# The mean of V from fp32 sums on GpSimd and one fp32 product, in a clustered-attention and MoE kernel

## The chip, the core and the metric

The kernel runs on one core of a Trainium2 chip. The metric is the device time of one execution in microseconds (us), the median of several runs. Engines are called as in the profile: PE is TensorE's matmul, PEld its weight load, DVE VectorE, ACT ScalarE, POOL GpSimd, SP SyncE, whose queue issues nearly all DMAs.

## The reference

Two batches of eight heads, 768 positions, head size 64. Queries and keys are each put into one of 16 clusters, and a query only sees keys of its own cluster. Where a query's cluster holds no key, every score is the same large negative number, and the softmax becomes the plain mean of V over all 768 positions. That is the mean in question.

```python
mask = q_assign[:, :, :, None] == k_assign[:, :, None, :]
scores = np.where(mask, scale * np.matmul(q, k.transpose(0, 1, 3, 2)), -1e9)
scores = scores - np.max(scores, axis=-1, keepdims=True)
attn = np.exp(scores)
attn = attn / (np.sum(attn, axis=-1, keepdims=True) + 1e-09)
x = np.matmul(attn, v)                 # then heads side by side: 1536 x 512
h = x @ w_in;   x = act1(h) @ w_out    # two feed-forward layers, 512 -> 2048 -> 512
h = x @ w2_in;  out = (s * relu(h) ** 2 + b) @ w2_out
```

## The kernel before

Heads go in eight pairs p (numbers 0 to 7), two heads of 64 columns side by side. The attention is a list of 96 slots t, six for each head, twelve for each pair; each slot handles 128 keys of a head. All engines run their instructions in the order in which the program issues them, and the order of a slot is written by hand in `slot(t)`: one half of the row maxima (`max_mm`, PE, L747), the DMAs of the slot (SP), the scores (`scores`, PE, L812 and L813), the other half of the maxima, the exponentials (`probs`: ACT makes `ph` in fp16 and `pf` in fp32 at L823 and L824, and POOL the rest `pl = pf - ph` at L826), the products with V of the slot before the last (`values(t - 2)`, PE, L842, which read `ph`, `pl` and V), then what the tables `steps` and `extra` hold for this slot. So `pl(t)` is wanted by PE two slots after its own.

V of a pair comes as `rv`, one buffer for all pairs (`load_v`, L475, in pool `rvp` with one buffer), 128 partitions of 2 heads x 6 pieces j x 64 columns. `scale_v` (L618) takes the largest magnitude, `peak_row` and `peak_all` (L630 to L651) carry it across partitions with a small fp32 product against the table `eye`, `scale_v2` makes the power of two `sc` and, with `iv` (L665), its inverse divided by 768. `split_v` (ACT, L673) and `split_v2` (DVE, L677) write V times `sc` as an fp16 pair `vh`, `vl`. When these are done, the one buffer `rv` is free, and the load of the next pair may go.

`mean(p)` stands in slot 12p + 7 (`PX`), behind that slot's `values`: twelve fp16 products of a 128x128 block of ones with `vh` and `vl` of the six pieces, summed in PSUM (L689, L690), and in the next slot two scaled copies by ACT, one for each head (L695). `no_match(p)` puts the mean where a query has no key, much later. `peak_all` of an odd pair stands in the same slot as the mean of the pair before, right behind it on PE. After slot 95 come the two feed-forward layers, products of 512 columns on PE to the end.

Of the kernel before, what the change touches and what calls it, by code (L numbers as in the profile page):

```python
# [8 lines left out]
F32 = mybir.dt.float32  # L9
# [4 lines left out]
ACTF = mybir.ActivationFunctionType  # L14
ALU = mybir.AluOpType
# [10 lines left out]
def clustered_attention_moe_kernel(  # L26
# [24 lines left out]
    nc = tc.nc  # L51
    B, H, S, D = q.shape
# [3 lines left out]
    J = S // 128  # L56
# [44 lines left out]
    def bank(kind, name):  # L101
        return banks[kind].tile([128, TB], F32, tag=kind, name=name)
# [3 lines left out]
    half, one, s_col, b_col, low = (cols[:, i:i + 1] for i in range(5))  # L106
# [251 lines left out]
    for n, w in enumerate(loadq[len(early):]):  # L358
        start, pace = PACES[w[0]]
# [47 lines left out]
    def attention(es, prep):  # L407
        def pool(name, bufs, stack=es):
            side = "left" if stack is prep else "right"
            return stack.enter_context(tc.tile_pool(name=name, bufs=bufs, side=side))  # L410
# [8 lines left out]
        acon = pool("acon", 1)  # L419
        ccon = pool("ccon", 1, prep)  # L420
        smp = pool("smp", 4)
        vp = pool("vp", 2)
# [3 lines left out]
        ident = acon.tile([128, 128], F32, name="ident")  # L426
        ones16 = acon.tile([128, 128], F16, name="ones16")
# [1 line left out]
        firsts = acon.tile([128, 128], F16, name="firsts")  # L429
        level = acon.tile([128, 2], F32, name="level")  # L430

        eye = acon.tile([2, 4], F32, name="eye")


        CW = 96 + 128 * HP
# [5 lines left out]
        raw, halves, sims, ohts, vt, heads, pr = {}, {}, {}, {}, {}, {}, {}  # L441
# [3 lines left out]
        def spare():  # L445

            if spares:
                spares.append(spares.pop(0))
                return bank(spares[-1], spares[-1] + "b")
            return bank("x", "xb")  # L450
# [174 lines left out]
        def peak_row(p):  # L625
            st = {}

            def pe():
                st["ps"] = spare()[0:2, 0:128]
                nc.tensor.transpose(st["ps"], vt[p][0], ident)  # L630

            def dve():
                mx = smp.tile([2, 1], F32, tag="pk", name="pk")
                nc.vector.tensor_reduce(out=mx, in_=st["ps"], axis=AX.X, op=ALU.max)
                ex = smp.tile([2, 1], I32, tag="ex", name="ex")

                nc.vector.tensor_scalar(
                    out=ex, in0=mx.bitcast(I32), scalar1=0x7F800000, scalar2=None, op0=ALU.bitwise_and
                )
                nc.vector.tensor_scalar(out=ex, in0=ex, scalar1=float(27 << 23), scalar2=None, op0=ALU.max)  # L640
                vt[p] = [ex.bitcast(F32)]

            return pe, None, dve

        def peak_all(p):
            st = {}

            def pe():
                st["ps"] = spare()[:, 0:4]
                ex = vt[p][0]  # L650
                nc.tensor.matmul(st["ps"], lhsT=ex.to_broadcast([2, 128]), rhs=eye, start=True, stop=True)  # L651

            def dve():
                scale_v2(p, st["ps"])

            return pe, None, dve

        def scale_v2(p, ex):

            sc = vp.tile([128, 2], I32, tag="sc", name="sc")  # L660
            nc.vector.tensor_scalar(
                out=sc, in0=ex[:, 0:2].bitcast(I32), scalar1=-1.0, scalar2=float(268 << 23), op0=ALU.mult, op1=ALU.add
            )
            iv = vp.tile([128, 2], F32, tag="iv", name="iv")
            nc.vector.tensor_copy(iv, ex[:, 2:4])  # L665
            vh = vp.tile([128, 2, J, D + 1], F16, tag="vh", name="vh")
            vl = vp.tile([128, 2, J, D], F16, tag="vl", name="vl")
            nc.gpsimd.memset(vh[:, :, :, D:D + 1], 1.0)
            vt[p] = [vh, vl, sc.bitcast(F32), iv, None]

        def split_v(p, e):
            vh, vl, scf, ivf, _ = vt[p]
            nc.scalar.activation(out=vh[:, e, :, 0:D], in_=raw[p, "v"][:, e], func=ACTF.Copy, scale=scf[:, e:e + 1])  # L673

        def split_v2(p, e):
            vh, vl, scf, ivf, _ = vt[p]
            nc.vector.scalar_tensor_tensor(  # L677
                out=vl[:, e], in0=raw[p, "v"][:, e], scalar=scf[:, e:e + 1], in1=vh[:, e, :, 0:D],
                op0=ALU.mult, op1=ALU.subtract,
            )  # L680

        def mean(p):
            st = {}

            def pe():
                vh, vl = vt[p][0:2]
                ps = st["ps"] = spare()[:, 0:2 * D].rearrange("p (h d) -> p h d", h=2)
                for j in range(J):
                    nc.tensor.matmul(ps, lhsT=ones16, rhs=vh[:, :, j, 0:D], start=(j == 0), stop=False)  # L689
                    nc.tensor.matmul(ps, lhsT=ones16, rhs=vl[:, :, j, :], start=False, stop=(j == J - 1))  # L690

            def act():
                mv = vp.tile([128, 2, D], F32, tag="mv", name="mv")
                for e in range(2):
                    nc.scalar.activation(  # L695
                        out=mv[:, e], in_=st["ps"][:, e], func=ACTF.Copy, scale=vt[p][3][:, e:e + 1]
                    )
                vt[p][4] = mv

            return pe, act  # L700

# [162 lines left out]
        def no_match(p):  # L864

            nm = spare()[:, 0:2 * J].rearrange("p (h j) -> p h j", h=2)
            nc.scalar.activation(out=nm, in_=heads.pop((p, "mx")), func=ACTF.Relu, scale=-1.0, bias=low)
            nc.vector.copy_predicated(
                out=heads[p, "x"],
                mask=nm.bitcast(I32).rearrange("p h j -> p j h")[:, :, :, None].to_broadcast([128, J, 2, D]),  # L870
                data=vt[p][4][:, None].to_broadcast([128, J, 2, D]),
            )

        def x_out(p, n):
            b, hp = divmod(p, HP)
            j0, j1 = PIECE[n]
            xs = slice(b * S + j0 * 128, b * S + j1 * 128)
            st = {}

            def pe():  # L880
                x = heads[p, "x"]
                ps = st["ps"] = spare()[:, 0:(j1 - j0) * 128]
                for j in range(j0, j1):
                    nc.tensor.transpose(
                        ps[:, (j - j0) * 128:(j - j0 + 1) * 128], x[:, j, :, :].rearrange("p h d -> p (h d)"), ident
                    )

            def act():
                nc.scalar.activation(out=xt_h[:, hp, xs], in_=st["ps"], func=ACTF.Copy)

            def dve():
                nc.vector.tensor_tensor(  # L892
                    out=xt_l[:, hp, xs], in0=st["ps"], in1=xt_h[:, hp, xs].bitcast(F32), op=ALU.subtract
                )

            return pe, act, dve
# [32 lines left out]
        steps, extra, mid, dmas = {}, {}, {}, {}  # L929

        def at(d, t, f, *a):
            d.setdefault(t, []).append((f, a))

        def step(t, x):
            steps.setdefault(t, []).append(x)

        for g in range(1, NH // 4):
            z = 24 * g
            for a, at_load, places in ((0, 46, PT[0:4]), (1, 34, PT[4:8])):
                p = 2 * g + a  # L940
# [10 lines left out]
        for p in range(NP):  # L951
            z = 12 * p
            zl, za, zs, zh, zg = PV[p % 2][0:3] + (PV[p % 2][3:5], PV[p % 2][5:7])
            if p != 1:
                at(dmas, z + zl + int(p == NP - 1), load_v, p)
            at(*((extra, z - 8) if p in (1, NP - 1) else (mid if p % 2 else extra, z + za)), scale_v, p)
            step(z + zs[0], peak_row(p))
            step(z + zs[1], peak_all(p))
            for e in range(2):
                at(extra, z + zh[e], split_v, p, e)  # L960
                at(extra, z + zg[e], split_v2, p, e)
            zx = PX[p % 2]
            step(z + zx[0], mean(p))
            if p < NP - 1:
                step(z + zx[1], x_out(p, 0))
                step(z + zx[2], x_out(p, 1))
# [91 lines left out]
        def turn2(p, nm, aside, *kinds):  # L1058
            spares[:] = kinds
            whole(turn(p, nm, 0, aside), turn(p, nm, 1, aside))  # L1060
# [58 lines left out]
        for x in (s0, s1):  # L1119
            x[0](((1, 1),))  # L1120
        s0[2]()
        s1[2]()
        nc.vector.tensor_copy(eye[:, 0:2], ident[0:2, 0:2])
        nc.vector.tensor_scalar(
            out=eye[:, 2:4], in0=ident[0:2, 0:2], scalar1=2.0 ** -14 / S, scalar2=None, op0=ALU.mult
        )
        turn2(2, "q", True, "s")
        turn2(2, "k", True, "m")
        warm(9)
# [41 lines left out]
        for e in range(2):  # L1171
            lead(J + e, ("ms", "sm")[e])
            split_v2(0, e)
# [9 lines left out]
    with tc.manual_schedule():  # L1183
        with ExitStack() as es, ExitStack() as prep:
            attention(es, prep)
        ff_pools(("wc", NWC))
        for n in range(TAIL, len(units) + 2):
            ff_step(n)
# [33 lines left out]
```

## Time and profile before

| | |
|---|---|
| median of 3 runs | 768.39 us (767.7 to 769.45) |
| profiled execution, span from first to last instruction | 766.2 us |
| mean granted TensorE clock | 0.997 of 2.4 GHz |
| PE busy | 747.7 us (98%), 5019 products |
| DVE busy | 483.3 us (63%) |
| ACT busy | 472.9 us (62%) |
| POOL busy | 318.3 us (42%) |

The page gives the profiled execution's span alone; the timed runs are about 2 us longer, which is what lies around the span. Shares of busy time are means over the attention (to about 240 us) and the feed-forward layers, which have different limits.

### The profile page before, as it was taken

Reading aid. Unit: us, or ns where it says so; the run is one execution under the profiler, and the core shown is the slowest. Engines: PE = TensorE matmul, PEld = TensorE weight load, DVE = VectorE, ACT = ScalarE, POOL = GpSimd, SP = SyncE. Lnnn points to the kernel's source line nnn. Section 1 sums busy time; section 2 is a strip of 40 time slices with the busy share of each in tenths; the row PEclk is TensorE's granted clock in tenths of the full one; section 3 lists DMA queues with packets and bytes.
Section 4 is the critical chain, followed back from the end, with each engine's and each line's share of the span. In section 5 each row is a group of like instructions: output and inputs, shape, how many; then the busy total and the mean of one; then the engine's idle time right before and its main releaser. Section 6 shows DMA issues by size and latency. Waiting matters only on the chain.

```text
span 766.2 us, 13218 instructions
## 1 busy us (share of the span) xinstructions
PE 747.7 (98%) x5019; PEld 622.5 (81%) x5019; DVE 483.3 (63%) x871; ACT 472.9 (62%) x949; POOL 318.3 (42%) x242
## 2 busy tenths in 40 slices
PE   8899999999999999999999999999999999999998
PEld 5678888988877787888888888888888888888886
DVE  6889898898887968885464349889932222222222
ACT  5389799898997777777466247866643333333332
POOL 4388688687885463555043004655630000000000
PEclk9999999999999999999999999999999999999999
DMA  9777657376511443443022003434400100010001
GB/s 199 166 154 167 142 111 174 93 162 165 134 55 58 137 138 111 137 138 111 0 84 83 0 1 119 136 103 142 133 1 1 55 1 1 0 56 1 0 1 55
DMA packets 59887, 67.52 MB, mean 88 GB/s; under 512 B 29008, under 2 KB 47536, under 8 KB 59824
## 3 DMA queue, kind: packets, MB, share of 16 engines
q1 hardware_dynamic: 59792, 66.63, 33.3%
q8 instruction: 39, 0.64, 0.4%
q14 instruction: 24, 0.20, 0.1%
q10 hardware_dynamic: 32, 0.05, 0.0%
HBM read 43.03 MB, written 3.15 MB: 60 GB/s over the span
## 4 chain that ended last, share of the span: by engine, by line
PE 83%; DVE 9%; DMA 3%; ACT 3%; issue 1%; SPq 0%; DVEq 0%; ACTq 0%
PE y L302 33%; PE h L241 32%; PE o L842 4%; PE m L747 3%; PE s L812 3%; PE s L813 3%; DVE rowmax L758 3%; PE xb L544 1%; DVE vl L677 1%; DMA rv<-in_v_dram 1%; DMA kb<-oht 1%; ACT ph L823 1%; DMA rk<-in_k_dram 1%; ACT pf L824 1%; PE xb L491 1%
## 5 line engine op out<-in xcount | busy, mean ns | idle before, releaser
L241 PE MATMUL h<-xt_h,w 128*128 128x512 f32 x768 | 252.9, 390 | 0.5 <-ACT w L179 0.4
L826 POOL TENSOR_TENSOR pl<-pf,ph 128x768 f16<-128x768 f32 x94 | 156.8, 1674 | 50.8 <-ACT pf L824 22.6
L241 PEld LDWEIGHTS h<-xt_h,w 128*128 128x128 f32 x768 | 144.1, 188 | 30.8 <-ACT w L179 0.8
L241 PE MATMUL h<-xt_l,w 128*128 128x512 f32 x384 | 149.6, 390 | 0.0
L277 POOL TENSOR_TENSOR gl<-g,gh 128x512 fp32r<-128x512 f32 x51 | 66.8, 1309 | 182.2 <-ACT gh L275 177.5
L275 ACT ACTIVATE gh<-g 128x512 fp32r<-128x512 f32 x96 | 60.4, 630 | 106.5 <-PE y L302 66.7
L823 ACT ACTIVATE ph<-s 128x384 f16<-128x384 f32 x192 | 102.1, 532 | 29.9 <-PE s L813 28.6
L302 PE MATMUL y<-gh,w 128*128 128x512 f32 x384 | 108.5, 390 | 1.2 <-DVE t L163 1.0
L758 DVE TENSOR_REDUCE rowmax<-m 128x1 f32<-128x384 f32 x180 | 95.4, 549 | 15.8 <-PE m L747 14.7
L302 PE MATMUL y<-w,gh 128*128 128x512 f32 x384 | 105.2, 389 | 0.0
L824 ACT ACTIVATE pf<-s 128x384 f32<-128x384 f32 x192 | 103.5, 539 | 0.0
L270 DVE TENSOR_SCALAR g<-g,cols 128x512 f32<-128x512 f32 x48 | 27.5, 573 | 100.8 <-ACT g L261 100.6
L302 PEld LDWEIGHTS y<-gh,w 128*128 128x128 f32 x384 | 72.0, 188 | 17.8 <-DVE t L163 1.4
L241 PEld LDWEIGHTS h<-xt_l,w 128*128 128x128 f32 x384 | 72.1, 188 | 14.9 <-DVE xt_l L892 0.2
L302 PEld LDWEIGHTS y<-w,gh 128*128 128x128 f32 x384 | 72.0, 188 | 15.0
L180 POOL TENSOR_TENSOR w<-t,w 128x512 fp32r<-128x512 f32 x64 | 83.1, 1309 | 0.0
L260 ACT ACTIVATE g<-h 128x512 f32<-128x512 f32 x48 | 28.6, 596 | 78.2 <-PE h L241 76.3
L747 PE MATMUL m<-kb,qb 80*128 80x384 f32 x180 | 68.4, 381 | 2.6 <-DVE rowmax L758 2.1
L277 DVE TENSOR_TENSOR gl<-g,gh 128x512 fp32r<-128x512 f32 x45 | 31.2, 693 | 62.5 <-ACT gh L275 62.5
L842 PEld LDWEIGHTS <-ph 128*128 128x128 f16 x1152 | 54.8, 98 | 19.0 <-issue 13.5
L812 PE MATMUL s<-qa,ka 128*128 128x384 f32 x192 | 66.7, 347 | 0.2 <-ACT pf L824 0.2
L813 PE MATMUL s<-qb,kb 128*128 128x384 f32 x192 | 65.0, 338 | 1.9 <-DMA qb<-mr 1.9
(195 smaller groups left out, 1304.4 us busy)
## 6 DMA issues: line engine op xcount, KB each, us to landing
raw<-in_moe_w_in_dram SPq DMA_DIRECT2D x32, 512.0 KB, 3.7
raw<-in_moe_w_out_dram SPq DMA_DIRECT2D x32, 512.0 KB, 3.3
rq<-in_q_dram SPq DMA_DIRECT2D x16, 192.0 KB, 4.4
rk<-in_k_dram SPq DMA_DIRECT2D x16, 192.0 KB, 4.9
rv<-in_v_dram SPq DMA_DIRECT2D x8, 384.0 KB, 5.3
out_dram<-o SPq DMA_DIRECT2D x12, 256.0 KB, 2.3
qb<-qh SPq DMA_DIRECT2D x14, 192.0 KB, 3.2
kb<-kh SPq DMA_DIRECT2D x14, 192.0 KB, 3.8
```

Of the source, the lines that this page charges most:

```text
L180: nc.gpsimd.tensor_tensor(out=l, in0=f, in1=h.bitcast(F32), op=ALU.subtract)
L241: nc.tensor.matmul(h_t[m, t, c], lhsT=w[:, kk * 128:(kk + 1) * 128], rhs=x[:, kk, tokens(t)], start=((n, kk) == H_PARTS[0]), stop=((n, kk) ...
L277: eng.tensor_tensor(out=gl, in0=g, in1=gh.bitcast(F32), op=ALU.subtract)
L302: nc.tensor.matmul(y[i], lhsT=ops[n][0], rhs=ops[n][1], start=(begin and n == 0), stop=(end and n == 2))
L747: nc.tensor.matmul(ps, lhsT=hd["qb"][0:NQ, j * 128:(j + 1) * 128], rhs=hd["kb"][0:NQ, n * S // 2:(n + 1) * S // 2], start=True, stop=True,)
L758: nc.vector.tensor_reduce(out=hd["m2"][:, j, n:n + 1], in_=mst.pop((u, n)), axis=AX.X, op=ALU.max)
L812: nc.tensor.matmul(ps, lhsT=hd["ka"][:, cs], rhs=hd["qa"][:, qs], start=True, stop=False)
L813: nc.tensor.matmul(ps, lhsT=hd["kb"][:, cs], rhs=hd["qb"][:, qs], start=False, stop=True)
L823: nc.scalar.activation(out=ph[:, qs], in_=ps, func=ACTF.Exp, scale=qk_scale)
L824: nc.scalar.activation(out=pf[:, qs], in_=ps, func=ACTF.Exp, scale=qk_scale)
L826: eng.tensor_tensor(out=pl, in0=pf, in1=ph, op=ALU.subtract)
L842: nc.tensor.matmul(o[:, j, 0:w], lhsT=lhsT[:, js], rhs=rhs[:, e, c, :], start=(c == 0 and j == 0 and x == 0), stop=(c == J - 1 and j == J ...
```

## The change

The mean no longer comes from the fp16 pair. `sum_v(p)` adds the six raw fp32 pieces of `rv` on POOL: five additions of 128 x 128 elements, the sum `vs` kept in place, in one buffer for all pairs. It stands in `extra` of slot 12p - 5, for pair 0 in slot 0, so behind that slot's `pl` in POOL's order. `mean(p)` stays in its slot, as a single fp32 product of a column of ones, broadcast to 128x128, with `vs`; ACT then makes one copy of 128x128 with the constant scale 1/768 in place of two. `iv` and its DVE copy go, and with them two of the four columns of `eye` and of `peak_all`'s product, and one small DVE instruction in the set-up.

```diff
-        eye = acon.tile([2, 4], F32, name="eye")
+        eye = acon.tile([2, 2], F32, name="eye")
...
-                st["ps"] = spare()[:, 0:4]
+                st["ps"] = spare()[:, 0:2]
...
-            iv = vp.tile([128, 2], F32, tag="iv", name="iv")
-            nc.vector.tensor_copy(iv, ex[:, 2:4])
...
+        def sum_v(p):
+            r = raw[p, "v"]
+            vs = raw[p, "vs"] = smp.tile([128, 2, D], F32, tag="vs", name="vs", bufs=1)
+            for j in range(1, J):
+                nc.gpsimd.tensor_tensor(out=vs, in0=vs if j > 1 else r[:, :, 0], in1=r[:, :, j], op=ALU.add)
+
         def mean(p):
...
-                for j in range(J):
-                    nc.tensor.matmul(ps, lhsT=ones16, rhs=vh[:, :, j, 0:D], start=(j == 0), stop=False)
-                    nc.tensor.matmul(ps, lhsT=ones16, rhs=vl[:, :, j, :], start=False, stop=(j == J - 1))
+                nc.tensor.matmul(
+                    ps, lhsT=one.to_broadcast([128, 128]), rhs=raw.pop((p, "vs")), start=True, stop=True
+                )
...
-                for e in range(2):
-                    nc.scalar.activation(
-                        out=mv[:, e], in_=st["ps"][:, e], func=ACTF.Copy, scale=vt[p][3][:, e:e + 1]
-                    )
+                nc.scalar.activation(out=mv, in_=st["ps"], func=ACTF.Copy, scale=1.0 / S)
...
+            at(extra, max(0, z - 5), sum_v, p)
...
-        nc.vector.tensor_copy(eye[:, 0:2], ident[0:2, 0:2])
-        nc.vector.tensor_scalar(
-            out=eye[:, 2:4], in0=ident[0:2, 0:2], scalar1=2.0 ** -14 / S, scalar2=None, op0=ALU.mult
-        )
+        nc.vector.tensor_copy(eye, ident[0:2, 0:2])
```

## Rows read from the trace of the kernel before

**Rows 1.** The page: busy time, share of the span and instructions of each engine.

```profile
PE 747.7 (98%) x5019; PEld 622.5 (81%) x5019; DVE 483.3 (63%) x871; ACT 472.9 (62%) x949; POOL 318.3 (42%) x242
```

**Rows 2.** Busy time by stretch: the attention's slots; us, busy (instructions), clock, DMA share, GB/s.

```profile
32.00:240.00 208.00, 200.38 (x2595) 174.77 (x2594) 178.76 (x388) 181.66 (x461) 160.86 (x104) 1.00 0.58 132
```

**Rows 3.** Groups by line and form: count | busy us, mean ns | idle before them.

```profile
L826 POOL TENSOR_TENSOR pl<-pf,ph 128x768 f16<-128x768 f32 x94 | 156.8, 1674 | 50.8 <-ACT pf L824 22.6 <-PE s L813 10.7 <-PE m L747 7.8
...
L689 PE MATMUL xb<-vh,ones 128*128 128x128 f16 x48 | 6.3, 220 | 0.0
...
L512 POOL TENSOR_TENSOR w<-rq,w 128x768 fp32r<-128x768 f32 x1 | 1.8, 1835 | 2.4 <-ACT rq L506 2.4
...
L665 DVE COPY iv<-xb 128x2 f32<-128x2 f32 x7 | 1.1, 150 | 0.0
```

**Rows 4.** The chain of waits around slots 19 to 21: start us, us, what.

```profile
75.33 0.06 PE xb L689
...
76.00 0.23 PE m L747
...
77.69 0.31 PE xb L651 x2
78.00 0.38 PE m L747
...
79.81 0.47 PE xb L491 x4
```

**Rows 5.** Timeline of slot 7: `ex` on DVE, then `peak_all` behind the mean.

```profile
50.39 0.14 DVE L640 TENSOR_SCALAR ex<-ex 2x1 int32<-2x1 int32 x1
...
50.58 0.29 PEld L651 LDWEIGHTS xb<-eye,ex 2*128 2x128 f32 x2
```

**Rows 6.** Timeline of POOL in the set-up: start us, us, instruction.

```profile
1.95 0.35 POOL L602 TENSOR_SCALAR_AFFINE_SELECT before<-before 128x128 f32<-128x128 f32 x1
2.38 0.45 POOL L606 TENSOR_TENSOR before<-before,ident 128x128 f32<-128x128 f32 x1
2.90 0.24 POOL L607 CAST firsts<-before 128x64 f16<-128x64 f32 x1
```

**Rows 7.** Timeline of POOL, `pl` of slots 6 and 7, then 8; in brackets its idle time.

```profile
48.96 3.37 POOL L826 TENSOR_TENSOR pl<-pf,ph 128x768 f16<-128x768 f32 x2 [1.50 <-PE s L813]
53.49 1.65 POOL L826 TENSOR_TENSOR pl<-pf,ph 128x768 f16<-128x768 f32 x1 [1.16 <-issue]
```

**Rows 8.** Timeline of PE: the first product that reads `pl` of slot 8.

```profile
56.03 0.19 PE L842 MATMUL o<-vh,pl 128*128 128x65 f16 x1
```

**Rows 9.** Timeline of POOL, `pl` of slots 66 and 67, then 68.

```profile
179.82 3.38 POOL L826 TENSOR_TENSOR pl<-pf,ph 128x768 f16<-128x768 f32 x2 [0.79 <-PE s L813]
183.90 1.65 POOL L826 TENSOR_TENSOR pl<-pf,ph 128x768 f16<-128x768 f32 x1 [0.70 <-PE m L747]
```

**Rows 10.** Timeline of PE: the first product that reads `pl` of slot 68.

```profile
186.42 0.19 PE L842 MATMUL o<-vh,pl 128*128 128x65 f16 x1
```

**Rows 11.** Timeline of POOL at the start of the slots, `pl` of slots 0 to 4.

```profile
35.95 1.65 POOL L826 TENSOR_TENSOR pl<-pf,ph 128x768 f16<-128x768 f32 x1 [9.57 <-ACT pf L824]
38.64 6.50 POOL L826 TENSOR_TENSOR pl<-pf,ph 128x768 f16<-128x768 f32 x4 [1.03 <-ACT pf L824]
```

**Rows 12.** Timeline of PE: the first product that reads `pl` of slot 1.

```profile
40.37 0.19 PE L842 MATMUL o<-vh,pl 128*128 128x65 f16 x1
```

**Rows 13.** Timeline of SP's queue: V of pair 1, and the row maxima of head 1.

```profile
38.05 0.83 SPq L475 DMA_DIRECT2D rv<-in_v_dram  x1
...
42.77 0.79 SPq L800 DMA_DIRECT2D qb<-mr  x1
```

**Rows 14.** Timeline of PE: its wait for that transfer.

```profile
46.72 0.44 PE L813 MATMUL s<-qb,kb 128*128 128x384 f32 x1 [1.70 <-DMA qb<-mr]
```

**Rows 15.** The chain of waits around slots 81 to 84.

```profile
209.42 0.95 DVE rowmax L758 x2
...
214.90 0.44 PE m L747
```

More of the change, by code (lines that the diff above doesn't have):

```diff
@@ L668, in scale_v2 @@
             nc.gpsimd.memset(vh[:, :, :, D:D + 1], 1.0)
-            vt[p] = [vh, vl, sc.bitcast(F32), iv, None]
+            vt[p] = [vh, vl, sc.bitcast(F32), None]
         def split_v(p, e):
-            vh, vl, scf, ivf, _ = vt[p]
+            vh, vl, scf, _ = vt[p]
             nc.scalar.activation(out=vh[:, e, :, 0:D], in_=raw[p, "v"][:, e], func=ACTF.Copy, scale=scf[:, e:e + 1])
         def split_v2(p, e):
-            vh, vl, scf, ivf, _ = vt[p]
+            vh, vl, scf, _ = vt[p]
             nc.vector.scalar_tensor_tensor(
@@ L685, in pe @@
             def pe():
-                vh, vl = vt[p][0:2]
                 ps = st["ps"] = spare()[:, 0:2 * D].rearrange("p (h d) -> p h d", h=2)
-                for j in range(J):
-                    nc.tensor.matmul(ps, lhsT=ones16, rhs=vh[:, :, j, 0:D], start=(j == 0), stop=False)
-                    nc.tensor.matmul(ps, lhsT=ones16, rhs=vl[:, :, j, :], start=False, stop=(j == J - 1))
+                nc.tensor.matmul(
+                    ps, lhsT=one.to_broadcast([128, 128]), rhs=raw.pop((p, "vs")), start=True, stop=True
+                )
             def act():
-                mv = vp.tile([128, 2, D], F32, tag="mv", name="mv")
-                for e in range(2):
-                    nc.scalar.activation(
-                        out=mv[:, e], in_=st["ps"][:, e], func=ACTF.Copy, scale=vt[p][3][:, e:e + 1]
-                    )
-                vt[p][4] = mv
+                mv = vt[p][3] = vp.tile([128, 2, D], F32, tag="mv", name="mv")
+                nc.scalar.activation(out=mv, in_=st["ps"], func=ACTF.Copy, scale=1.0 / S)
             return pe, act
@@ L870, in no_match @@
                 mask=nm.bitcast(I32).rearrange("p h j -> p j h")[:, :, :, None].to_broadcast([128, J, 2, D]),
-                data=vt[p][4][:, None].to_broadcast([128, J, 2, D]),
+                data=vt[p][3][:, None].to_broadcast([128, J, 2, D]),
             )
```

## The prediction

> **What bounds the kernel now.** I read the page's busy shares first: PE is busy for 98% of the span and POOL for 42% [rows 1], which looks like an exchange of dear time for cheap time. That share is a mean over two stages, so I read the stretches next. All of the change lies in the 208 us of the slots, and there POOL is busy for 160.9 us, 77%, while PE is busy for 200.4 us, 96% [rows 2]. Then the groups by form: of POOL's work there, 156.8 us are the 94 instructions that make `pl`, 1.67 us each [rows 3]. A slot lasts 208 / 96 = 2.17 us, so POOL has about half a microsecond of room in a slot, and PE waits for its result two slots later. Last, the timelines around the places where additions are put: when `pl` of the slot ends, when the next one starts, and when PE first reads that next one. That is the room which a burst of POOL work has before PE stands still. The chain of waits tells whether PE sets the pace there: in most slots it runs over PE alone, as around slot 19 [rows 4].
>
> **What the additions cost.** The trace has one POOL addition of 128x128 in fp32: 0.45 us, with the dependent instruction behind it starting 0.52 us after it started [rows 6]. The five additions form such a chain, each reading the sum that the one before wrote: 4 x 0.52 + 0.45 = 2.53, taken as 2.5 us for a pair. From below: a POOL addition over 768 columns takes 1.835 us [rows 3], 0.31 us for a sixth of the columns if nothing were fixed, so 1.55 us for five. From above: 0.52 us and another gap such as the 0.08 us between the end of L602 and L606 [rows 6], 0.60 each, 3.0 us. I take 2.5 since L606 has the shape, type and dependence of the new instruction.
>
> The Trainium skill, GPSIMD Engine Reference, section 3.1, gives about 2.6 cycles per element for a two-input operation at 1.2 GHz; an estimate from this page is 0.28 us for 128 columns, 1.4 us for five, which gives the first rival's time below. The trace agrees with the slope and not with the total: L606 and L512 differ by 1.38 us over 640 columns, 2.16 ns each, but at 128 columns the row has 0.18 us more than the slope alone.
>
> **Where they stand.** `sum_v(p)` is issued behind `pl` of slot t = 12p - 5, at once ready (V landed long ago, and the mean that last read `vs` is finished on PE before that `pl` ends). `pl` of slot t + 1 queues behind it on POOL, and PE's `values` of t + 1 behind that. For pair 1, t = 7: `pl` ends at 48.96 + 3.37 = 52.33, the next one starts at 53.49 and ends at 55.14 [rows 7], and PE reads it at 56.03 [rows 8]. The room is 1.16 + 0.89 = 2.05 us. With 2.5 us PE stands 0.45 us. The same reading gives 2.06 and 2.07 for pairs 3 and 5, and 2.01 for pairs 2 and 4: these five lose 0.43 to 0.49 each, 2.3 us together. For pair 6, t = 67: 183.90 - 183.20 = 0.70, and 186.42 - 185.55 = 0.87 [rows 9, 10], room 1.57, loss 0.93. Pair 7 has 1.58, loss 0.92; but there the chain runs over DVE from 209.42 to PE's maxima at 214.90 [rows 15], so a late PE is partly made good, and I count 0.3. The pl two slots on has more room in each of the seven places, so nothing is lost twice.
>
> **Pair 0.** The additions follow `pl` of slot 0, which ends at 37.60 [rows 11], and end at 40.1. Two things wait. `pl` of slot 1 starts at 40.1 and not 38.64, ends at 41.75, and PE wanted it at 40.37 [rows 11, 12]: 1.4 us late. And `rv` has one buffer, which the additions still read: SP issued the load of pair 1's V at 38.05 [rows 13] and must now stand until 40.1, 2.05 us, with the loads of Q and K and the row maxima of head 1 (`mr`, issued at 42.77) behind it in its queue. PE waits 1.70 us for just that transfer [rows 14], so it has no cover; the 1.4 us of late `pl` vanish inside the same wait, and the later of the two counts. How much of 2.05 us reaches PE no row shows: nothing, if data issued earlier still fill the DMA engines, or all of it. I take the middle, 1.0 us, as these engines are neither idle nor full (0.58 of the stretch [rows 2]). From pair 1 on the additions are done many slots before the next load of V, so SP waits no longer there.
>
> **What PE saves.** The twelve products last from 75.33 to 76.00, 0.67 us [rows 4]; of the two kinds the first alone has 48 instructions [rows 3]. One fp32 product stands in the trace as two passes: `peak_all` with four columns takes 0.31 us, and the maxima behind it 0.38 us where they take 0.23 behind the mean [rows 4]; 124 more columns in two passes at the rate of fp32 transposes (0.47 / 4 = 0.12 us per 128 columns) make 0.31 + 0.15 + 0.24 = 0.70 us at most. From below it is two passes, 0.24 us. I take 0.6, nearer to the product of the same kind, so a mean saves 0.07 us, between -0.03 and 0.43. Most of it would be lost in any case. In pairs 0, 2, 4 and 6 the mean stands before a `peak_all` that waits for `ex`: `ex` ends at 50.53 and `peak_all` starts at 50.58 [rows 5], in all four places 0.05 us after it, so the mean fills a wait. In pairs 1, 3 and 5 the mean is in the very slot whose `pl` the additions follow; when PE comes earlier to `values`, it waits longer for POOL. Only pair 7's mean, in slot 91, gives its 0.07 us back: 0.1.
>
> **The small edits.** ACT makes one copy in place of two, and DVE loses a copy of 0.15 us for each pair [rows 3]. Both lie beside PE's work: where PE runs the chain their ends are not what PE waits for, and where DVE runs it the copies are too short to matter: overlapped with their neighbours, less than 0.15 us each. The narrower `eye` and the set-up instruction count for nothing: `peak_all` is as long as its two passes. If PE's cover were gone, all DVE copies together would be 8 x 0.15 = 1.2 us of gain.
>
> **The sum.** 1.0 (pair 0) + 2.3 (pairs 1 to 5) + 0.9 (pair 6) + 0.3 (pair 7) - 0.1 = 4.4 us. The profiled execution's span, 766.2 us, becomes 770.6; the runs shown have a median 2.2 us above that span, so 772.8 us. The feed-forward layers are the same work, on PE, started later.
>
> **The rivals.** First, on the other side: the additions hide. It is decided by their length: with at most 1.57 us for five (0.31 each), no `pl` is late, and PE's savings stay in pairs 1, 3, 5 and 7: up to 4 x 0.43 = 1.7 us, less half of the 39.15 - 38.05 = 1.1 us by which the first load is late: 768.4 - 1.7 + 0.55 = 767.2 us with the cheapest product, 769 with the dear one. For it speaks the slope of POOL's rows; against it the one row of the same shape. Chance 0.08.
>
> Second, the additions nearly fit: 0.41 us each, 2.0 us together. Pairs 1 to 5 lose nothing, pair 6 0.4, pair 7 none, pair 0 half of 1.55: 1.1 us with the 0.1 off, 769.5 us, which is within 0.2% of before (1.5 us, about what a measurement of this kernel tells from no change). For it: the input is the same memory, and L606 is a single row; against: its length would have to be a fifth off. Chance 0.15.
>
> Third, more is lost: 0.60 us for each addition, and the whole delay of SP's queue reaches PE. Then pair 0 costs 2.55, pairs 1 to 5 five times 0.93 to 0.99 (4.8), pair 6 1.4, pair 7 0.8: 9.5 us, 777.8 us. For it: the pieces are strided halves of 64 columns where L606 reads 128 in a row, and PE's 1.70 us of waiting [rows 14] are on that queue. Against: nothing in the rows shows POOL slower for it. Chance 0.17. The forecast itself has 0.60.
>
> **Range and chances.** The low end takes in most of the second rival and leaves the first out; the high end goes most of the way to the third: 769.3 to 777.0 us. Slower by over 0.2%: the forecast, the third and a small part of the second, 0.80. Within it: the rest of the second and a little of the first, 0.15. Faster: 0.05.
>
> **What the profile will show.** Five POOL additions of some 0.45 us in eight places, 0.52 apart; `pl` of slots 8, 20, 32, 44, 56, 68 and 80 starting right behind them, and PE idle before L842 with POOL as releaser, 0.4 to 0.9 us in each; SP's load of V for pair 1 at about 40.1; the mean as two passes; the feed-forward layers unchanged. The prediction is wrong if the additions are 0.4 us or less, if PE's lateness in these places is given back by waits that follow, or if `mr` of head 1 lands no later than before.

## The result, and the profile after

The changed kernel takes 777.55 us (median of four runs, 776.92 to 778.15) where the kernel before took 768.05 beside it: a ratio of 1.0113, interval 1.0096 to 1.0131. That is 8.7 us slower by the ratio, 9.5 us by the two medians. The forecast was 4.4 us slower, 772.8 us in a range of 769.3 to 777.0; the time lies 0.55 us above its end, about twice the forecast loss. The profiled span is 775.0 us, 8.9 us longer than before (8.8 by the page's rounded figures), and it is this difference that is divided up below.

The page after, busy time and share of each engine; PE does less and POOL more than in [rows 1]:

```profile
PE 746.7 (96%) x4939; PEld 620.5 (80%) x4939; DVE 490.4 (63%) x862; ACT 472.1 (61%) x941; POOL 339.0 (44%) x282
```

Two views tell most. First the waits of PE in the stretch of the slots, 32 to 248 us, of the kernel after (what it waited for: us in total, times, longest):

```profile
PE o L841 <- POOL pl L825: 5.3, 9, 1.3
PE m L746 <- DVE rowmax L757: 5.1, 9, 1.5
...
PE xb L651 <- DVE ex L640: 1.3, 4, 0.3
PE s L812 <- DMA qb<-mr: 1.0, 1, 1.0
```

and the same view of the kernel before, where PE had no wait for POOL's `pl` at all:

```profile
PE m L747 <- DVE rowmax L758: 2.1, 6, 0.7
PE s L813 <- DMA qb<-mr: 1.9, 2, 1.7
```

The first wait is the forecast one. The second, on DVE's row maxima, has grown by 3 us, and nothing in the forecast speaks of it. The second view, groups by line and form of the kernel after, shows which instruction on DVE became dearer:

```profile
L675 DVE SCALAR_TENSOR_TENSOR vl<-rv,sc,vh 128x384 f16<-128x384 f32 x16 | 20.6, 1284 | 0.0
...
L825 POOL TENSOR_TENSOR pl<-pf,ph 128x768 f16<-128x768 f32 x94 | 160.2, 1714 | 36.0 <-ACT pf L823 23.4 <-PE s L812 6.4 <-PE s L811 2.6
...
L684 POOL TENSOR_TENSOR vs<-vs,rv 128x128 f32<-128x128 f32 x32 | 14.7, 458 | 2.5
L684 POOL TENSOR_TENSOR vs<-rv 128x128 f32<-128x128 f32 x8 | 3.6, 455 | 0.0
```

An addition takes 0.46 us, 0.01 above the row that the forecast took it from [rows 6]. The `pl` group, 156.8 us in [rows 3], is 160.2 us now. The `vl` group is `split_v2`, which the change does not touch; before, the same sixteen instructions took 13.8 us:

```profile
L677 DVE SCALAR_TENSOR_TENSOR vl<-rv,sc,vh 128x384 f16<-128x384 f32 x16 | 13.8, 861 | 0.0
```

Where that happens is seen best around pair 1. POOL's timeline after, which answers to [rows 7] (start, us, instruction, idle time before it in brackets):

```profile
49.64 3.37 POOL L825 TENSOR_TENSOR pl<-pf,ph 128x768 f16<-128x768 f32 x2 [0.72 <-PE s L812]
52.97 0.45 POOL L684 TENSOR_TENSOR vs<-rv 128x128 f32<-128x128 f32 x1
53.50 2.06 POOL L684 TENSOR_TENSOR vs<-vs,rv 128x128 f32<-128x128 f32 x4
55.52 1.66 POOL L825 TENSOR_TENSOR pl<-pf,ph 128x768 f16<-128x768 f32 x1
57.11 0.17 POOL L666 MEMSET vh<- 128x12 f16 x1
57.17 3.60 POOL L825 TENSOR_TENSOR pl<-pf,ph 128x768 f16<-128x768 f32 x2
61.12 3.56 POOL L825 TENSOR_TENSOR pl<-pf,ph 128x768 f16<-128x768 f32 x2 [0.35 <-PE s L812]
```

The five additions last from 52.97 to 55.56, 2.59 us, and behind them POOL is without a gap until 60.77. DVE's two `vl` instructions of that pair, after:

```profile
57.42 1.83 DVE L675 SCALAR_TENSOR_TENSOR vl<-rv,sc,vh 128x384 f16<-128x384 f32 x1
...
61.16 2.02 DVE L675 SCALAR_TENSOR_TENSOR vl<-rv,sc,vh 128x384 f16<-128x384 f32 x1
```

and before:

```profile
56.74 0.98 DVE L677 SCALAR_TENSOR_TENSOR vl<-rv,sc,vh 128x384 f16<-128x384 f32 x1
...
59.85 0.61 DVE L677 SCALAR_TENSOR_TENSOR vl<-rv,sc,vh 128x384 f16<-128x384 f32 x1
```

POOL beside them before:

```profile
55.66 1.65 POOL L826 TENSOR_TENSOR pl<-pf,ph 128x768 f16<-128x768 f32 x1 [0.43 <-PE s L813]
...
60.19 5.20 POOL L826 TENSOR_TENSOR pl<-pf,ph 128x768 f16<-128x768 f32 x3 [0.86 <-PE m L747]
```

Before, the first `vl` begins 1.08 us behind the start of a `pl`, so late in it, and the second 0.34 us ahead of one. After, each begins just behind the start of a `pl` on POOL (57.17 and 57.42; 61.12 and 61.16) and ends some 0.4 us after that `pl`, 1.65 us long, is through. In PE's timeline after, this is the pair of waits, first for the late `pl` and then for the row maxima that stand behind `vl` in DVE's order:

```profile
57.24 0.20 PE L841 MATMUL o<-vh,pl 128*128 128x65 f16 x1 [0.37 <-POOL pl L825]
...
63.70 0.45 PE L746 MATMUL m<-kb,qb 80*128 80x384 f32 x1 [1.46 <-DVE rowmax L757]
```

The start of PE's scores in each slot, after minus before, gives the account. It rises or falls in these steps (us):

| where | forecast | in the trace after |
|---|---|---|
| pair 0 (slots 0 to 10, of this one execution; see below) | 1.0 | 0.69 |
| additions of pairs 1 to 5 (slots 11, 23, 35, 47, 59) | 2.3 | 0.55, 0.64, 0.55, 0.66, 0.50: 2.90 |
| additions of pair 6 (slot 71) | 0.9 | 1.09 |
| additions of pair 7 (slot 83, and 84) | 0.3 | 1.03 - 0.21 = 0.82 |
| row maxima behind `vl` of pairs 1 and 3 (slots 13, 37) | none | 1.51, 1.51: 3.02 |
| the mean's product, pairs 1, 3, 5 and 7 | -0.1 | 3 x (-0.42 + 0.34) - 0.44 = -0.68 |
| other steps (+0.33, -0.10, -0.58, +0.19 at slots 60, 61, 66, 72; less than 0.1 each elsewhere) | none | about -0.25 |
| from slot 95 to the feed-forward layers | none | 0.4 |
| behind the last product | none | 0.90 |
| sum | 4.4 | 8.9 |

The 0.33 at slot 60 is the same thing once more and smaller: PE waits 0.15 us just before its scores there for row maxima behind a `vl` of pair 5 that takes 1.83 us. A step of 0.31 to 0.43 us stands there in every kernel below that has the whole burst, and not with one, with three or with spread additions. The -0.58 at slot 66 stands in all of them within 0.05, with one addition too, so it is not of the burst; what it is was not followed.

The feed-forward layers are the same work: the last product begins at 762.07 us before and at 770.05 after, 7.98 us later, as the first ones do.

### The profile page after: what moved, and what is told of

The parts are those of the page before. It is cut to its first block, busy times and chain, and to the rows that moved or that the text cites. A ratio compares the mean times of both kernels' runs of the same rounds, so it can differ in the third digit from the quotient of the medians.

```text
span 775.0 us, 13077 instructions
## 1 busy us (share of the span) xinstructions
PE 746.7 (96%) x4939; PEld 620.5 (80%) x4939; DVE 490.4 (63%) x862; ACT 472.1 (61%) x941; POOL 339.0 (44%) x282
## 4 chain that ended last, share of the span: by engine, by line
PE 77%; DVE 10%; ACT 5%; POOL 3%; DMA 2%; issue 1%; SPq 0%; DVEq 0%; POOLq 0%; ACTq 0%
PE y L302 32%; PE h L241 30%; PE o L841 4%; PE m L746 3%; PE s L812 2%; PE s L811 2%; DVE rowmax L757 2%; POOL pl L825 2%; DVE vl L675 1%; ACT ph L822 1%; ACT pf L823 1%; PE xb L544 1%; PE idle L1075 1%; POOL vs L684 1%; DMA rk<-in_k_dram 1%
## 5 line engine op out<-in xcount | busy, mean ns | idle before, releaser
L825 POOL TENSOR_TENSOR pl<-pf,ph 128x768 f16<-128x768 f32 x94 | 160.2, 1714 | 36.0 <-ACT pf L823 23.4
L822 ACT ACTIVATE ph<-s 128x384 f16<-128x384 f32 x192 | 98.8, 515 | 36.4 <-PE s L812 34.7
L823 ACT ACTIVATE pf<-s 128x384 f32<-128x384 f32 x192 | 99.6, 519 | 3.4 <-POOL pl L825 3.0
L841 PEld LDWEIGHTS <-ph 128*128 128x128 f16 x1152 | 55.1, 98 | 20.0 <-issue 13.8
L841 PE MATMUL o<-vh,pl 128*128 128x65 f16 x576 | 62.2, 194 | 6.0 <-POOL pl L825 5.3
L841 PE MATMUL o<-vh,ph 128*128 128x65 f16 x576 | 64.6, 196 | 2.3 <-DVE x L859 2.3
```

Of the source, the lines that this page charges most:

```text
L822: nc.scalar.activation(out=ph[:, qs], in_=ps, func=ACTF.Exp, scale=qk_scale)
L823: nc.scalar.activation(out=pf[:, qs], in_=ps, func=ACTF.Exp, scale=qk_scale)
L825: eng.tensor_tensor(out=pl, in0=pf, in1=ph, op=ALU.subtract)
L841: nc.tensor.matmul(o[:, j, 0:w], lhsT=lhsT[:, js], rhs=rhs[:, e, c, :], start=(c == 0 and j == 0 and x == 0), stop=(c == J - 1 and j == J ...
```

## The experiments

Ratios are against the kernel before, on the same chip, with 95% intervals.

**One addition, and three.** In the changed kernel:

```diff
-            for j in range(1, J):
+            for j in range(1, 2):     # e1; range(1, 4) in e2
```

The mean is then that of two or of four of the six pieces.

> One of the five additions is left in each pair, so the mean is of two of the six pieces of V; the product with ones and the single copy stay as changed. The first theory holds that the loss comes from a 2.6 us burst on POOL, which makes pl late for PE directly (about 4.5 us) and pushes later pl into the time of split_v2 on DVE (about 3 us more). By it 0.46 us of POOL work is under every room in the seven places (1.57 us at least), the loss goes, and what is left is what PE saves by the short product: 766.5 to 768.1 us, no wait of PE for POOL before L841. The rival, that the fp32 product itself or the waits around it cost the time, expects 775 us or more. A second rival, that each addition costs its share, expects 768 + 9.5/5 = 770 us.

> Three of the five additions in each pair (mean of four of the six pieces), a burst of 2 x 0.535 + 0.46 = 1.53 us. If the loss has a threshold at the rooms read from the trace of before (1.57 us at pairs 6 and 7, 2.01 to 2.07 us at pairs 1 to 5), PE still waits for POOL in none of the seven places, pair 0 costs about half a microsecond, and the collisions with split_v2 are fewer: 767 to 770 us. If every addition costs its share of the 9.5 us, 768 + 5.7 = 773.7 us. If the product costs the time, 775 us or more.

With one addition 767.72 us, 0.9986 (0.9970 to 1.0003); with three 768.82 us, 1.0005 (0.9986 to 1.0023). With one, PE waits for `pl` once, 0.2 us; with three twice, 0.4 us in all, and the `vl` group takes 13.7 us in both, as before (13.8). Both times lie where the burst was expected to leave them. The fp32 product, the single copy and the small edits are in both kernels, so what the change costs in the slots lies in the last two of five additions. Three last 2 x 0.535 + 0.46 = 1.53 us, just under the room of the tightest place, 1.57.

**The additions alone.** The kernel before, with `sum_v` in its place and its result unused:

```diff
+        def sum_v(p): ...
...
+            at(extra, max(0, z - 5), sum_v, p)
```

> The kernel before with the five additions of each pair put in at the same places, their sum read by nobody; the mean still comes from the twelve fp16 products. The burst theory expects the whole loss, and a little more since PE's saving (0.4 us at pair 7, little elsewhere) is gone: 776.5 to 778.5 us, with the same waits before L842. The rival, that product and copy cost the time, expects 768 to 770 us.

777.34 us, 1.0119 (1.0092 to 1.0146), as expected: the whole loss, without any other part of the change. PE waits 4.8 us for `pl` and 5.0 us for row maxima, and `vl` takes 20.2 us.

**Pair 0 early.** The additions of pair 0 in the set-up, right behind `scale_v(0)`, so that `rv` is read early:

```diff
-            at(extra, max(0, z - 5), sum_v, p)
+            if p:
+                at(extra, z - 5, sum_v, p)
...
         scale_v(0)
+        sum_v(0)
```

> The changed kernel with the additions of pair 0 moved into the set-up, where POOL is idle from 26 to 36 us, so that neither pl of slot 1 nor SP's load of V for pair 1 waits for them. The shift of PE's scores between the two traces after head 1's maxima have landed is 0.69 us; if that is all of pair 0's price: 776.9 us. If the delay of SP's queue by 2.1 us is carried further than that, 775.5 to 776.4 us. If pair 0 costs nothing in the end, 777.5 us.

776.65 us, 1.0106 (1.0083 to 1.0128), which its interval does not part from the changed kernel, nor from any of the three outcomes that were expected. SP's load of V is back at 38.18 us. PE still waits for `mr`, by its timeline in this kernel:

```profile
46.84 0.64 PE L812 MATMUL s<-qb,kb 128*128 128x384 f32 x1 [1.59 <-DMA qb<-mr]
```

**The additions spread.** Pair 0 early as above, and for the others two, one, one and one addition in four slots:

```diff
+                for n, js in enumerate(((1, 2), (3,), (4,), (5,))):
+                    at(extra, z - 5 + n, sum_v, p, js)
```

> The changed kernel with all five additions kept but not in one burst: pair 0's in the set-up, the others' two behind pl of slot 12p - 5 and one behind pl of each of the next three slots. If the burst is the cause, two additions (1.0 us) and then 0.46 us at a time fit into POOL's gaps and the room behind them, split_v2 is disturbed little, and the time is that of the run with one addition, 767 to 769 us. If POOL's sum of work is the cause (20.6 us more in the stage, however spread), 773 us or more.

770.51 us, 1.0021 (1.0000 to 1.0042), 1.5 us above the 767 to 769 that were expected of the burst, and well under the 773 expected of the sum of POOL's work. The same 40 additions cost about 6 us less than with pair 0 early alone when no place in the slots holds more than two: PE's waits for `pl` come to 0.2 us, and `vl` to 14.8 us. In the trace the span is 1.6 us longer than before, and 0.9 of that lie behind the last product, which is taken up further down.

**What makes `vl` long.** Two kernels change what POOL does beside it. In the first, the changed kernel makes `pl` of slots 9 to 11 and 33 to 35 by filling it with zeros, four fills of half a tile, so that POOL is as busy but reads nothing; the low part of the probabilities is missing in these six slots. In the second, eleven fills of an unused tile stand in the kernel before in place of the additions.

```diff
+            if t in (9, 10, 11, 33, 34, 35):
+                for h in range(2):
+                    nc.gpsimd.memset(pl[:, h * S // 2:(h + 1) * S // 2], 0.0)
+                    nc.gpsimd.memset(pl[:, h * S // 2:(h + 1) * S // 2], 0.0)
+            else:
+                eng = nc.vector if t in VPL else nc.gpsimd
```

```diff
+            for _ in range(11):
+                nc.gpsimd.memset(idle_t, 0.0)
```

> The changed kernel, but pl of slots 9 to 11 and 33 to 35, which the burst pushes into the time of split_v2 of pairs 1 and 3, is not computed: POOL fills it with zeros in four memsets of half a tile, which write and don't read (the low part of the probabilities is left out in these six slots). If the long split_v2 (1.8 and 2.0 us in the place of 1.0 and 0.6) come from two instructions that both read SBUF through one interface, they fall back to 0.6 to 1.0 us although POOL is as busy, PE's two waits of 1.5 us for the row maxima behind them go, and the time is 774.3 to 775 us. If any POOL work beside them does it, 777.5 us as before.

> The kernel before, with eleven memsets of 128x128 at the places of the additions, between 2.2 and 3.0 us of POOL work that reads nothing; the sum of V isn't made and rv isn't held. If it is the length of the burst that matters and not what it reads, pl of slots 8, 20, 32 and so on is late as with the additions, the displaced pl disturbs split_v2 as before, and the time is 774 to 780 us by its length. If the additions' own reading matters, it stays below 771 us.

The first took 774.14 us, 1.0082 (1.0052 to 1.0113). Its `vl` of pair 1, on DVE's timeline:

```profile
57.26 0.60 DVE L675 SCALAR_TENSOR_TENSOR vl<-rv,sc,vh 128x384 f16<-128x384 f32 x1
60.87 0.61 DVE L675 SCALAR_TENSOR_TENSOR vl<-rv,sc,vh 128x384 f16<-128x384 f32 x1
```

and POOL's fills, the first and the last of twelve, with at most 0.06 us between one and the next:

```profile
56.97 0.43 POOL L826 MEMSET pl<- 128x384 f16 x1
...
61.63 0.42 POOL L827 MEMSET pl<- 128x384 f16 x1
```

The additions stand, the step of +0.52 us at slot 11 stands, and the step of 1.5 us at slot 13 is gone, as is that at slot 37; PE's waits for row maxima are back at 2.0 us. The fills are also shorter than a `pl`, so one might think that `vl` only waited less. It did not wait at all: the first `vl` begins 0.29 us into a fill of 0.43, the second 0.07 into one of 0.42, and each takes what a `vl` with nothing beside it takes (0.61). So it is POOL's reading that makes `vl` long. By the intervals of the times alone this kernel is not quite parted from the changed one; the steps are.

The second took 774.60 us, 1.0081 (1.0052 to 1.0110). I had expected the same collision behind a burst that only writes, since the displaced `pl` are as before. It did not come: the two `vl` of pair 1 took 0.60 and 0.61 us:

```profile
56.30 0.60 DVE L677 SCALAR_TENSOR_TENSOR vl<-rv,sc,vh 128x384 f16<-128x384 f32 x1
...
60.16 0.61 DVE L677 SCALAR_TENSOR_TENSOR vl<-rv,sc,vh 128x384 f16<-128x384 f32 x1
```

beside these of POOL:

```profile
51.83 2.83 POOL L686 MEMSET vs<- 128x128 f32 x11
54.62 1.64 POOL L832 TENSOR_TENSOR pl<-pf,ph 128x768 f16<-128x768 f32 x1
56.20 0.15 POOL L668 MEMSET vh<- 128x12 f16 x1
56.26 3.77 POOL L832 TENSOR_TENSOR pl<-pf,ph 128x768 f16<-128x768 f32 x2
60.19 5.35 POOL L832 TENSOR_TENSOR pl<-pf,ph 128x768 f16<-128x768 f32 x3 [0.15 <-PE s L819]
```

The pair of `pl` took 3.77 us where an undisturbed pair takes 3.37: here POOL waited. The second `vl` begins 0.03 us ahead of its `pl`. The first begins 0.04 us behind the recorded start of its `pl` and still did not wait (so too in pairs 3 and 5, 0.02 and 0.03 behind, 0.60 us each), so a few hundredths between recorded starts do not tell who comes first. The fill in front of that `pl` runs until 56.35, past the start of `vl`. My reading is that `pl` began to read only then; no run shows it. This kernel also gives a second dose: with a burst of 2.83 us the steps of the seven places are 0.75, 0.79, 0.75, 0.79, 0.71, 1.22 and 1.22 us, and burst less room is 0.78, 0.82, 0.77, 0.82, 0.76, 1.26 and 1.25.

**A longer burst.** If what counts is which of the two begins first, more work on POOL can make the kernel faster. In the changed kernel:

```diff
+            if p in (1, 3):
+                nc.gpsimd.memset(vs, 0.0)
+                nc.gpsimd.memset(vs, 0.0)
```

and beside it the changed kernel once more.

> The changed kernel with more work in the burst of pairs 1 and 3: two memsets of 128x128 ahead of the additions, about half a microsecond. If a split_v2 that starts just behind a displaced pl waits for all of it, while one that starts just ahead makes pl wait, half a microsecond of delay moves pl of slots 9 and 33 behind split_v2: the first split_v2 of pairs 1 and 3 falls from 1.83 to about 0.6 us, PE's waits of 1.5 us for the row maxima shrink or go, the direct waits grow by 0.5 each, and the kernel with more work is 0.5 to 2 us faster than the changed one. If lateness on POOL simply adds up, it is 1 us slower.

> The changed kernel once more, on the same chip as the run with the longer burst, so that the two can be compared: 777 to 778 us.

The longer burst took 775.17 us, 1.0083 (1.0061 to 1.0105), the changed kernel again 777.38 us, 1.0114 (1.0085 to 1.0143): the medians are 2.2 us apart in favour of more work, a little more than expected. The intervals against the kernel before overlap, but eight of the ten runs with the longer burst lie under the lowest of the eight of the changed kernel beside it (775.99). The traces are plainer. With the longer burst, POOL around pair 1:

```profile
53.80 0.20 POOL L684 MEMSET vs<- 128x128 f32 x1
...
54.88 2.06 POOL L687 TENSOR_TENSOR vs<-vs,rv 128x128 f32<-128x128 f32 x4
...
58.54 3.54 POOL L828 TENSOR_TENSOR pl<-pf,ph 128x768 f16<-128x768 f32 x2
62.47 3.71 POOL L828 TENSOR_TENSOR pl<-pf,ph 128x768 f16<-128x768 f32 x2 [0.39 <-PE s L815]
```

and DVE:

```profile
58.28 0.67 DVE L675 SCALAR_TENSOR_TENSOR vl<-rv,sc,vh 128x384 f16<-128x384 f32 x1
62.45 0.61 DVE L675 SCALAR_TENSOR_TENSOR vl<-rv,sc,vh 128x384 f16<-128x384 f32 x1
```

The first `vl` begins 0.26 us ahead of its `pl` and takes 0.67 us; in the changed kernel it begins 0.25 us behind and takes 1.83. The second begins 0.02 us ahead and takes 0.61 us; in the changed kernel it begins 0.04 us behind and takes 2.02. The direct steps grow to 1.05 and 1.07 us, and those of 1.5 us at slots 13 and 37 are gone; in the repeat of the changed kernel they are there again (1.51 and 1.50).

## Why the prediction was half the size

**What held.** The direction, and the mechanism that it names: `pl` displaced by a burst longer than the room in front of PE's next read. The loss is burst less room in every place: 2.59 less 2.05, 2.01, 2.06, 2.01, 2.07, 1.57 and 1.58 is 0.54, 0.58, 0.53, 0.58, 0.52, 1.02 and 1.01, against steps of 0.55, 0.64, 0.55, 0.66, 0.50, 1.09 and 1.03. The additions were taken at 2.5 us, 0.09 short, since the dependent start is 0.535 us apart and not 0.52. Pairs 1 to 6 cost 3.99 us and not 3.2, which is 0.8 of the 4.5 us missed; six times 0.09, some 0.5, is the longer burst, and the rest is steps a little above burst less room. The rooms read from the trace of before were right to a few hundredths. Their fate is shown by the doses too: 1.53 us is nearly free, 2.83 us costs what the rooms say.

**The step that failed** is the sentence "The pl two slots on has more room in each of the seven places, so nothing is lost twice." It followed the late `pl` to PE alone, and so put the wait for row maxima behind `split_v2` at nothing. In pairs 1 and 3 the late `pl` of the following slots begins just ahead of `split_v2` on DVE, which then takes 1.8 to 2.0 us and not 0.6 to 1.0; the row maxima queue behind it, and PE stands 1.46 us at slot 13 for them. That is 3.0 us for the two pairs. The first `vl` of pairs 2 and 4 grew too, from 0.61 to 1.40 and 1.42 us, without a step of its own. That it is POOL's reading, and when it begins, was shown from both sides: with fills in its place, or with the burst made 0.5 us longer, the step is gone. The trace of before had the sign of it in the same group of sixteen, whose mean was 0.86 us where one with nothing beside it takes 0.61; I had read past it.

The Trainium skill, SBUF — State Buffer, section "Who interferes with whom", says that a VectorE instruction with two inputs in SBUF contends with a GpSimd instruction that reads SBUF, not with one that only writes it, and that issue order decides which of the two blocks. The traces agree: 0.60 us beside fills, 2.02 us begun 0.04 us behind a `pl`, 0.61 us begun 0.02 us ahead of one; the 0.60 us begun 0.04 us behind a recorded start, in the kernel with fills for the additions, fits only if that start is not the issue that counts.

**Pair 7** was counted at 0.3 us because the chain of waits ran over DVE there [rows 15]. 1.03 us were lost and only 0.21 given back: 0.5 us missed. Here the chain over another engine at one point did not measure how much a delay shrinks.

**Pair 0** was taken at 1.0 us, between 0 and 2.05. What was forecast of the queue came: SP's load of V and the row maxima, after, answering to [rows 13],

```profile
40.19 0.39 SPq L475 DMA_DIRECT2D rv<-in_v_dram  x1
...
43.98 0.79 SPq L799 DMA_DIRECT2D qb<-mr  x1
```

the load 2.14 us later than before and `mr` 1.21, since the issues between became shorter. PE goes on at 47.39 us, 0.67 later than in [rows 14]. But the profiled executions do not let this stand as its price: in the repeat of the changed kernel `mr` is issued at 44.30 and PE goes on at 46.67, no later than before, with the additions early and `mr` issued at 43.24 it goes on at 46.84 after a 1.59 us wait, and with the additions alone, `mr` issued at 45.76, at 48.78. In the changed kernel PE first stands 1.29 us for the late `pl` of slot 1, and part of this comes back since the wait for `mr` is then 1.03 us and not 1.70. That first step, 1.4 to 1.7 us at slot 4, is in every kernel with a whole burst in slot 0; what is left of it by slot 10, against the kernel before, runs from -0.44 to 2.06 us, while the two kernels with early additions stand at 1.67 and 0.12. Slot 0 itself already begins 0.73 us earlier to 1.59 us later than before. One profiled execution differs from the next by more than the delay of the issue. The early additions took 0.9 us off the changed kernel's time, within the intervals. Pair 0's price stays open.

**What PE saves.** The product was taken at 0.6 us, with 0.24 as the lower bound. After:

```profile
77.87 0.47 PE L691 MATMUL xb<-vs,cols 128*128 128x128 f32 x2
78.10 0.44 PE L746 MATMUL m<-kb,qb 80*128 80x384 f32 x1
```

The next product begins 0.23 us behind its start: the lower bound, and a saving of 0.42 to 0.44 us where a mean does not fill a wait. That it fills one in pairs 0, 2, 4 and 6 was right: the wait for `ex`, 1.3 us in four places, is the hole that it left. In pairs 1, 3 and 5 it is given back, but not where the forecast put it: 0.34 of the 0.42 us already in the next slot, before `pl` is wanted. Only pair 7's 0.44 lasted to slot 95, and 0.4 us were lost between there and the feed-forward layers; I did not follow what of it belongs to the change.

**The rivals.** The time is nearest the third rival's 777.8 us, but not by its way: an addition took 0.535 us and not 0.60, and in the profiled execution 0.67 us of SP's 2.14 reached PE. The first two needed additions of 0.41 us or less; the trace has none under 0.45.

**Behind the last product** 0.9 us came that no step foresaw. The last 7 us of DMA after, by queue (packets, MB, share of 16 engines), and the last stores with the median us to landing:

```profile
q1 hardware_dynamic: 576, 1.05, 40.8%
q14 instruction: 1, 0.01, 0.3%
...
out_dram<-o SPq DMA_DIRECT2D x4, 256.0 KB, 3.1
```

and before:

```profile
q1 hardware_dynamic: 576, 1.05, 45.5%
...
out_dram<-o SPq DMA_DIRECT2D x4, 256.0 KB, 2.1
```

One packet of the instruction queue falls among the last stores, and these land 1.0 us later. It is so in all eight profiled kernels that were made from the changed one (it and its repeat, with one addition, with three, with pair 0 early, spread, with fills for `pl`, with the longer burst); in the two made from the kernel before (the additions alone, fills in their place) and in that itself there is no such packet and the median is 2.1 us. That the packet holds the stores up is my reading; no run moved it by itself, and why it falls there was not tried.

## What to carry to other kernels

When work is put on an engine with room in its slots, read the room from the timeline up to the next reader, and compare it with the length of the whole burst: here three additions in a place were nearly free, five cost burst less room in each, and five spread over four slots cost little. Then follow what the burst displaces to every engine, not only to its reader: a late GpSimd instruction that reads SBUF (the on-chip memory that both engines read) may come to begin just ahead of a two-input VectorE instruction that used to pass in front of it, and what queues behind that one pays. A share of busy time (POOL 42%) shows neither.

## What the runs showed that I had not expected

- A VectorE `split_v2` of 0.61 us took 1.83 to 2.02 us where it began 0.04 to 0.25 us behind the start of a GpSimd subtraction of 1.65 us, and 0.61 us where it began 0.02 us ahead of one; then a pair of GpSimd's instructions took 3.71 us and not 3.37. Behind a fill, 0.02 to 0.04 us behind the subtraction's recorded start was still early enough: 0.60 us. Two fills of 0.20 us more on GpSimd in two places made the kernel 2.2 us faster by the medians.
- An fp32 product of 128x128 by 128 columns, two passes, held PE for 0.23 us, from its start to that of the next product, in this stream, where twelve fp16 products of the same shape held it for 0.67 [rows 4].
- A chain of GpSimd additions in place, 128x128 in fp32, starts every 0.535 us; one takes 0.46 us.
